# Twelve strips of the dead normalised input as feed-forward tile homes, output rows spread between the next tiles, and a new written-out order

## The chip, the core and the metric

The kernel runs as one program on one core of a Trainium2 chip. The metric is the device time of one execution in microseconds (us). All five engines take part: TensorE (PE, with its weight loads shown as PEld), VectorE (DVE), ScalarE (ACT), GpSimd (POOL), and SyncE (SP), whose queue issues nearly all DMAs.

## The reference

A layer norm without scale feeds an attention block and a gated feed-forward block, and both are added to the input:

```
x = A_x                                   # 1 x 2048 x 512, bf16
xn = (x - mean) / sqrt(var + 1e-5)
q, k, v = split(xn @ A_wqkv)              # 32 heads of 16
o = softmax(q k^T / 4) v                  # 2048 x 2048 scores per head
gate, up = xn @ B_W_gate, xn @ B_W_up     # 512 -> 1792 each
return x + o @ A_wo + (max(gate, 0) * up) @ B_W_down
```

## The kernel before

**Tiling.** The 2048 rows are four chunks of 512 (`c4`), the 32 heads four groups of eight (`gg`), each in two halves (`ee`), the keys sixteen tiles of 128 (`kt`). One key step is one (`c4`, `gg`, `ee`, `kt`): scores of 128 keys against 512 queries for four heads. Of the 512 key steps, 359 go through ScalarE: each gives two units, 718 in all. `score` (L1289) makes the two score tiles of a unit in two PSUM banks, and one activation of 128x1024 (L1365) takes the exponential into a slot of `ring`. There are two such pairs of banks, so the scores of unit u+2 wait for the exponential of unit u. The other 153 key steps are "quads" (`quad`, L1312, placed by the table `QUAD_AT`): VectorE turns the scores into integers that, read as bf16, are approximate exponentials (L1320), and VectorE (L1339) or GpSimd (L1335) makes two shifted copies; all three patterns are multiplied with v. `pv_stream` (L1244) does the products with `v_aug`.

**TensorE's groups.** Nearly every product is split into two row halves of the array (64 rows each) and four column strips of 32. Four matmuls of 64x512 on one half are one group; four weight loads go before it unless the half still holds the same weights. Groups of the two halves run side by side. Line L250 is the helper that emits every one of these matmuls, so they are told apart by their tiles.

**Feed-forward and rows.** `glu` (L992) makes one tile of the feed-forward's hidden layer: a chain of eight groups for `up`, eight for `gate`, and two VectorE operations (L1016, L1020); the result goes to one of `NHS` = 20 slots of `hT`, pool `P_h` (L608). There are 14 such tiles (`ft`) for each chunk, 56 in all. `out_rows` (L1034) makes 128 output rows: a chain of 28 groups over all 14 tiles of the chunk and `W_down`, eight more over the attention output and `W_o`, then the residual. It needs all 14 tiles of its chunk, and frees them when the last of the four rows has read them. The normalised, transposed input `xnT` (128 x 4 x 2048, bf16) is read by all projections; block `c4` of its columns is not read again after the last projection of chunk `c4`. Late in the program `resid` (L1030) keeps two fp32 residuals of the last chunk in it.

**Order.** The jobs (projections, hidden tiles, rows) get due times from a list: all the tiles of a chunk, then its four rows, then the next chunk's tiles:

```
            for ft in range(FT):
                ...
                seq.append(ffn[ft])
                if ft in shared[c4]:
                    seq.append((0, GN, lambda s, c4=c4, ft=ft: glu(c4 + 1, ft, s), W_LEAD + 2))
            seq += rows
```

Half of the tiles of a chunk can be made together with the same tiles of the chunk before it (`shared`), because they use the same weights. But the order in which each engine runs its operations is not worked out when the program is built: `PLAN` is a packed table of `PLAN_OPS` = 8248 entries, which `Graph.run` (L324) unpacks into five queues, with the slot of every tile. `Graph.emit` then sets the semaphore waits. Each engine runs its queue strictly in that order; a wait at the head of a queue holds up all behind it.

Of the kernel before, what the change touches and what calls it, by code (L numbers as in the profile page):

```python
# [16 lines left out]
S = 2048  # L17
# [26 lines left out]
ROW_AT = 20  # L44
XBANKS = (0, 1, 2, 3)
# [82 lines left out]
    "v#>-|tRzVEh^;*em;WkE095*CSm<HqH|`M|cr09qT?N{VqVkBF%{%E!F2OyVSrjJo#C@^#5)-#ki(ELx!R42&{H1*&2Hxz52r$buahFFFHO%CC#9Q)JX4)?UB?Bn-@h~$EIv~rA8_Cs;WrYXK$Nit2"
    "M!^`XNhfIu!$pr-LS8yEID~)F1h<%6rs(#5!hPxRm9Y^lkGYG%5gr*R0~OLCGBU+!z=V64=^WYo$tfJMfyPTKzOG}v;bF$wOvcRc*~FY;Bv>(tiF*u~8(XJvKX15AfN<jhZuJo_&2ULV6kSIO6u07Z"
    "n^5&Yev|jYSj=N$RJvkR9J6dQw^K}4WnknQ2KJbTo4lwq%O)-%r<f?UuuDHk&%DjiSK&Se(yeb+R>Tduswg~lX?yeb(aF4Nkg+hqF8uHqwZ!ZoHmb)Pd?OPS5BUuDmX8s2!)cF~_zloVDiYqnivk~q"  # L130
    "nY1CwOy{3m@(zy-tptie8y<@zOv?m=nS1CyhNEu=B`7eOk-4-{f*<_M5>EDG7OrJlj3<qH<B}A0Uq6ShIT>w0_7VdV7WXDQb<H4KFK}%NhI8+iw?X?D-P<nA;$d8|bq!xzx2@%?Juea2d0J6Ycihz4"
    "iKpttb}qMXVl_42%G{@Q45=jhvlSWL=1(da;oV)g$rSi7X|g-_={ghMqMLJ*p}1~7rOW*c)nvS?_#*193-N&Jm2bY<vBgpM1wl8Rg-!aJs>hOTHhssvVvX}uy4D`TRBeJ=Dnik}C}X4+x2a?83x)z8"
    "P7M7D-$pVbhF-Mp(9NeUoO!Rm(9_&TEIgIe=U=4H*8F8n=~jp=p$ePY^|cgh5n-d%d3{m#82#JSWxiUqOr$1lsdSSV4fZs9w5f$mrt#t2l1_2~v;V<-Ua~WEtC}S<>(DK_7H`2Y3_dto2=#_e`(*Vt"
    "g9R+@W;o|D>5$AY83nqH+ATj!ijo4rE1_gF@^%OKB%gf8QYqHkoEu9rL-W|xonmNwAueE>v%JypMjKYVr8c%?2{)Cy)N9<j!4?E=hFLc`6E;RMR`D1WWsO<B25P)&-fH?P6*#ko0@_pi<kkdX=$0AY"
    "b-5+Vm{;o?c`)6VVKthH$2WqAMUB=5`+#hhw3ZGx!(`SvynFdD{aNE?a4o!<6(z;2ck1!(p?il87~_pKDf!TwTKRHY?HQuc1c<PXTbt^pKioTXnWmT_=C;>JnKGs*-f6>xf;lFcv!dN{GbE;9x6M>u"
    "tGxmi+^fa8t?L>ypru?bvh&uSabXVK-jem|O>Rzxu+2K$8f>l3FN?r5-n!Fl)?9I`7NeRin;X0Yo9|xdypb~dl5M=V+J(jQTxUwEcI)dZ+$){!Ga*kcp}qZ)f7yfok84w%BYZKC*;~J_!F>T9pD$Lg"
    "wKR=+qeb4{Dc*a8A$73TabdB#?_Tq~fZmp;6JjBm8p}iYu<YymJXI&NkD1(em|@|J+X7_G_r|e=PXlpp!?%=(#HU<JN3zp?4wWi>+}2KQ8>O0Xl~f(sUZ(aVEw7$1k1xLH;Kqe{xT0`h;%p~f+y@f="
    "#p_;p@l;sh|G&hSV$NGd7UwJG5s<F|7}p*}VZKms-w?tjWty|PhuKd*OpyhXdll~h=qn<#3DUrn>{8^QZP1{H!?fBMj-cq?QyE3E23c=Ev+<-S)iIUHH1ypZowzl}*=oWjam0RH`z&R)mpDwI*-m<l"
    "-F07|Ft;`PiA9;#$$+)7uNRn3de2=9BdmiRk7BV6Yy}`&q(#PxSMb=*&x}+UozfUkpjaJ1w?-jDoZ4;U)~S*uq%4Y&t;FXmw^OfTQ-I1BptV7t`zB_<CwadlFOM}``;H!TQ?!_AHAhZ!d{$sJG>=UO"
    "d1G(1JfA4^wjMd;d86r_>22g_Vaiy^I@dFhV5&6Ejjp4Z+@^aMF;t8<-d594yhLR-ck95_cb;iKjx_V)v%mzJUGsU*?d;;frr#{In(EdXI=L}cf7WRB=e`4Acp1*BBi%UrvQE+zZg1!O|IYQTpS{dx"  # L140
    "$|c2ys{fY|+}6kKyz0d?-RgE28MgEzPu+w6uRGfN0k;H!ZxG?BdGL$7?I$6yW7*dV?1#Dh3u@)c7oS1c(QXGk=cxuQ+j&6h-r^gM6#U;x*8FCdAKuy4dLFh;>zmGX?)#j=D_LNDBBJ|t@SUU^D|oNG"
    "M@eQ@eZ#68w``rwHXEfvi<LiPH*@+_yo0?-A76~WHm_}JMuA-z!_p~&aCK4lrdEM9=c{hTMrZa<ldK$CM^8M}NNqn`u~d7itaI<-d#ZGCdp^DL$d(S9+jf{4kHI>%GGj?J$jx(H&OFv==beibWBj$w"
    "78R@SS;vST>oWzj$$7kEnRwbf@3So{=Ky95OXf)@^Du9dvMExXS<|k0<X}IAlAVehW?Lud<{+jh7R`IfT(=$E8T`X+XIOfwdXXSEWS_y&1}vCIM1iOJ>_oTb3-hBKZYg`8#b$f-wtZ`&P<-0ME;qcN"
    "W?8gsJ#CF~)`xSjv$|!Ki4?1)n`5H)Lm1hi%mXT)q~c!=S2k+09pR?_e1xYyd9&$m`-j1)`nmT5Q!hmM7jusHsZ>W%itn>jbJnr5lwFbXR39v*5(Zx?Z`((whHU3H;p`pAQk}(k&-)al+T16Uzxcc&"
    "RfzZ(AKAh7nJ)KDNvYgVb!h87$m7PG<dye!D)1ho=wEzNXdB<`r}MtHl4=^TO)p;6<^2>uNeu~KRCV||_LpmkzZsDFzXwh@Kfi|x##s@lx~l4@OK6(^Csp@P!L#(5pL!pe@iZ&^#O;|ikDrJBIxmN5"
    "HyIw}rPmy8`iIeXaYL}@CCkXz)iBM;{=sc}|0W6mIT%9TF{GhwRDQm6LOGnKJ#hi`S>=^LuFA(Mvz@dGeWyQ22CA=YyP#~k7n$CqnbBT%{vHFAOSuPp9hmHNyRHGnpJhl1czXvZ@+yt?%5lBqEqc@K"
    "@_R-$`0WU;wk3kD(v2yNW0SWbxDXIBDo1;b7GB<w?bB-Q9d#?VO&GuTs1t4fJ`RoPZvgPB*F*%hUk^NU?IE`537o-SWpLtorXIj=Ps8zN+UJ=nlmRZTja;7+{Vi~5Y3r40x)<%XeXmzN98`{cN^-j0"
    "fu(`{F5Suacfe8S^3L<yulNl(wMc8P4gG2hurmG8JuJLbLm*xomQu&X;_m{dn{NBjHD;vVzeC}x6wC2>@8r@So!kn<J)Xg@6mqj))2D1m*$32$)E&z^YR$--<((F{UF=7%#r{*^W`WB^)n9=rxgPDQ"
    "F$@^z!spLh&jO=dZ*wFEJR1U(Y>?tmH#HqWacd6enr7=R0b|ywiw~4apw}i8|0^YJlC~U($=(JN-4uw6IC5O?5kC!R<Qj;_tJ^PH2Q(dosa@yM#i(sl`-DB99ZKc8l^^L6{ssoejoj}(hq;xHhVQ6^"
    "_5pg|S+BPP37FY?QgYyj1fXJ)BYg^Rfc%(<&jVNH1S(I%uS3T#j`HgrA#VMU2H#w!2$TX^6=9d%MP>qZS7G_}f_d(=7<26m(DGjP$!Okc4p1W4ec74QbrSd!{oSsj4VwVRdydASi3GN%(=P%CS<j0o"  # L150
    "qTL6w)EqZzLh0SQs^94KFA(XcPe$L*<VWkzepAqE7K&c}2FC}vV`HG6Am~QB%XaR1QsDYv?@RkPd<^>Ncj7jXv(%C@IFk`*=y)IU-v1AvKKx>v&Fn*oeTeSgM<OYN(9`)Ckl3u<!gZ}xk%K6#Vy#gU"
    "I1&1jn=L^UW&8*l)zuDGIZBsR9xyB!`rrEMp{s#r&*D(54m(AV>8qbYI$+wI?(-cnYbag$_xa&Tb2r(Mh;lKpQOjfIQSmve&VC$#`hSwjiNJwgJ5cBMN<iMFXup&%Kl%L-jQ<@d_z8Y*6AAG74x!Sm"
    "uL*G&F^+oEi2YR#CL$9D=Jv+qq2q^AEk6l-h#U`5n2O?7*0d=RJ0I+-yQgywAonsP^`ugKg3E1cj2+gZLqW=9w!GJztl_!Rny2R8gwsHUuP0-G`!3aI*um=Bvh5Q^S~t6!<HC*RC9@JVSsU(PwD@j("
    "p4)=6P-GbTC*70t$y20NHHuP~E{kIpclj6DAGf4<bSi<*UjhH&{PpCLDSkD9;aVrm?}o7Zi0g%{EjBh=*NVb_16iDp@UjqX@!wgOqUBdJ10$;3DEKyD;m?nFmfBQ~>|HBh9b**}7{a~*Hq6ooU}`_S"
    "Z$Z_Y2?v`#IpU(ro10o;Rg(>r-R(%xTMXj=u68THwj?KWJJDcUeQZwB)C{gFK+>Ojc6@f?M=G4MC%*MNx#caDTD$&J7hTozP|EK8MG$HdUnlS%;)Rq3o1BfdeD$bwe9jvM?jGanno|M@RON2gyaHuB"
# [382 lines left out]
def bass_parallel_sum__mha_block__glu_gated_reglu__prompt_kernel(  # L538
# [14 lines left out]
    with ExitStack() as es:  # L553
# [864 lines left out]
```

## Time and profile before

| what | value |
|---|---|
| median of 3 runs (all) | 685.31 us (685.06, 685.31, 686.58) |
| profiled execution, its own time: span from first to last instruction | 684.2 us |
| granted TensorE clock, mean | 0.999 |
| PE busy | 675.6 us (99%), 22262 matmuls, 19654 weight loads |
| ACT busy | 666.8 us (97%), 718 exponentials of 128x1024 |
| DVE busy | 598.5 us (87%) |
| POOL busy | 499.8 us (73%) |
| DMA, mean | 52 GB/s |

The times of the runs are taken without the profiler; the profiled execution is a further one, and its span is 1.1 us below the median of the runs. Busy times of TensorE are pipelined and their ends are modelled, so that 99% does not mean that the array is full. The exponentials of ScalarE also overlap in the profile: the next one begins before the one before has written its end. So the distance between their starts is read below, not their duration.

### The profile page before, as it was taken

What the parts mean: (1) busy time and instruction counts of PE and PEld (TensorE: products, weight loads), DVE (VectorE), ACT (ScalarE), POOL (GpSimd) and SP (SyncE); (2) the same over time, 40 slices, a digit from 0 to 9 for tenths busy, and PEclk for the clock granted to TensorE, in tenths of its full rate; (3) what the DMA queues carried; (4) which work ended last, traced back from release to release, by engine and by line L of the source; (5) the groups of instructions that cost most, each with busy time, mean ns of one, the idle gap of its engine ahead of it and who ended that gap; (6) DMA issues with size and microseconds to landing.
All of it is one profiled execution on the core that took longest, in us unless ns stands there. A gap on an engine that the chain in (4) does not pass through costs nothing.

```text
span 684.2 us, 45020 instructions
## 1 busy us (share of the span) xinstructions
PE 675.6 (99%) x22262; PEld 345.9 (51%) x19654; DVE 598.5 (87%) x1012; ACT 666.8 (97%) x730; POOL 499.8 (73%) x507
## 2 busy tenths in 40 slices
PE   8999999999999999999999999999999999999998
PEld 4455454545555554554444455554554455555543
DVE  9958899999989787999999788889998887988875
ACT  6999999999999999999999999999999999999994
POOL 3323768678688778887587886888878868787792
PEclk9999999999999999999999999999999999999999
DMA  7430220113122021212101022120202012131011
GB/s 216 57 75 12 58 77 27 33 55 91 56 65 66 5 77 34 69 41 63 35 23 31 10 78 63 38 69 5 56 27 61 25 53 62 44 86 42 22 36 54
DMA packets 55940, 35.86 MB, mean 52 GB/s; under 512 B 19336, under 2 KB 51784, under 8 KB 55752
## 3 DMA queue, kind: packets, MB, share of 16 engines
q1 hardware_dynamic: 55464, 32.71, 17.4%
q8 instruction: 164, 2.69, 1.6%
q10 hardware_dynamic: 288, 0.26, 0.1%
q14 instruction: 24, 0.20, 0.1%
HBM read 26.35 MB, written 2.35 MB: 42 GB/s over the span
## 4 chain that ended last, share of the span: by engine, by line
PE 75%; ACT 18%; DVE 5%; issue 1%; DMA 0%; POOL 0%; ACTq 0%
PE ps L250 75%; ACT ring L1365 18%; DVE stats L726 1%; DVE qd L1320 1%; DVE xn_sb L739 1%; DVE v_aug L876 0%; DMA x_sb<-in_A_x_dram 0%; DVE qT L952 0%; DVE mv L727 0%; ACT xn_sb L1164 0%; DVE qd L1339 0%; DVE xnT L780 0%; POOL rstd L721 0%; DVE xnT L1075 0%; DVE kT L869 0%
## 5 line engine op out<-in xcount | busy, mean ns | idle before, releaser
L1365 ACT ACTIVATE ring<-ps 128x1024 bf16<-128x1024 f32 x718 | 660.4, 1141 | 2.9 <-PE ps L250 2.5
L1335 POOL TENSOR_TENSOR qd<-qd,ints 128x512 int32<-128x512 int32 x446 | 450.5, 1041 | 143.8 <-DVE qd L1339 73.2
L250 PE MATMUL ps<-qT,kT 64*32 64x512 bf16 x8192 | 448.7, 374 | 1.3 <-DVE qd L1320 0.4
L1320 DVE TENSOR_SCALAR qd<-ps 128x512 int16<-128x512 f32 x612 | 396.7, 685 | 51.9 <-PE ps L250 49.0
L250 PE MATMUL ps<-qd,v_aug 64*32 64x512 bf16 x3672 | 263.0, 375 | 1.1 <-issue 0.9
L250 PE MATMUL ps<-ring,v_aug 64*32 64x512 bf16 x2872 | 236.5, 374 | 0.1
L1300 PEld LDWEIGHTS <-kT 64*32 64x32 bf16 x7584 | 151.1, 92 | 126.6 <-issue 32.6
L1272 PEld LDWEIGHTS <-v_aug 64*32 64x32 bf16 x4544 | 108.7, 91 | 75.6 <-issue 20.4
L250 PE MATMUL ps<-xnT,wgs 64*32 64x512 bf16 x1792 | 137.6, 374 | 0.0
L250 PE MATMUL ps<-xnT,wus 64*32 64x512 bf16 x1792 | 136.4, 374 | 0.0
L250 PE MATMUL ps<-Wd,hT 64*32 64x512 bf16 x768 | 59.0, 375 | 0.0
L810 PEld LDWEIGHTS <-wgs 64*32 64x32 bf16 x1792 | 43.1, 91 | 31.5 <-issue 7.4
L810 PEld LDWEIGHTS <-wus 64*32 64x32 bf16 x1792 | 43.2, 91 | 29.8 <-issue 7.6
L1339 DVE TENSOR_SCALAR qd<-qd 128x2048 int16<-128x2048 int16 x83 | 56.1, 690 | 2.3 <-PE ps L250 2.2
L810 PEld LDWEIGHTS <-hT 64*32 64x32 bf16 x1792 | 40.2, 92 | 28.2 <-issue 4.2
L250 PE MATMUL ps<-Wv,hT 64*32 64x512 bf16 x512 | 45.7, 375 | 0.0
L250 PE MATMUL ps<-Wk,hT 64*32 64x512 bf16 x512 | 42.8, 375 | 0.4 <-DVE qd L1320 0.3
L1020 DVE SCALAR_TENSOR_TENSOR hT<-ps,up_sb 128x512 bf16<-128x512 f32 x56 | 38.4, 685 | 4.6 <-PE ps L250 4.2
L1016 DVE COPY up_sb<-ps 128x512 f32<-128x512 f32 x56 | 38.4, 685 | 3.1 <-PE ps L250 2.5
L250 PE MATMUL ps<-Wo_p,x_sb 64*32 64x512 bf16 x480 | 40.2, 374 | 0.6 <-issue 0.5
L250 PE MATMUL ps<-xnT,Wq 64*32 64x512 bf16 x480 | 36.2, 375 | 0.0
L250 PE MATMUL ps<-xnT,Wk 64*32 64x512 bf16 x480 | 35.0, 374 | 0.3 <-DVE xnT L780 0.3
(70 smaller groups left out, 263.8 us busy)
## 6 DMA issues: line engine op xcount, KB each, us to landing
rb<-rec_scr SPq DMA_DIRECT2D x31, 256.0 KB
wus<-in_B_W_up_dram SPq DMA_DIRECT2D x38, 128.0 KB, 2.8
wgs<-in_B_W_gate_dram SPq DMA_DIRECT2D x38, 128.0 KB, 3.3
xr_sb<-in_A_x_dram SPq DMA_DIRECT2D x16, 128.0 KB, 2.6
qT<-qf SPq DMA_DIRECT2D x120, 16.0 KB, 2.6
out_dram<-xn_sb SPq DMA_DIRECT2D x14, 128.0 KB, 2.0
x_sb<-in_A_x_dram SPq DMA_DIRECT2D x8, 128.0 KB, 2.8
x_sb<-oT SPq DMA_DIRECT2D x60, 16.0 KB, 2.5
```

Of the source, the lines that this page charges most:

```text
L250: return e.add_instruction(mybir.InstMatmult(name=e.bass.get_next_instruction_name(), engine=mybir.EngineType.PE, ins=[e.lower_ap(x), e.lo ...
L726: G.op("DVE", 580, lambda e, m=m: e.bn_stats(stats[:, m, :], xs(m)), reads=[t_xm[m]], writes=[t_st], prio=pr, order=last_xn if m == 4 else ())
L739: G.op("DVE", 320, lambda e, m=m, t=t_n: e.tensor_scalar(xn_sb[:, t.slot, :], xs(m), mv[:, m, 0:1], rstd[:, m:m + 1], op0=ALU.subtract, op ...
L810: e.ldweights(w()[rows, 32 * j:32 * j + 32], tile_position=(rows.start, 32 * j))
L1016: G.op("DVE", 603, lambda e: e.tensor_copy(up_sb[:, tup.slot, :], bank_of(tu)), reads=[tu], writes=[tup], prio=-590)
L1020: G.op("DVE", 603, lambda e: e.scalar_tensor_tensor(out=hT[:, th.slot, :], in0=bank_of(tg), scalar=0.0, in1=up_sb[:, tup.slot, :], op0=ALU ...
L1272: e.ldweights(vs(j), tile_position=(64 * half, 32 * j))
L1300: e.ldweights(ks(m), tile_position=(64 * half, 32 * m))
L1320: G.op("DVE", 601, lambda e, j=j, tx=tx: e.tensor_scalar(qd[:, tq.slot, 512 * j:512 * j + 512], ps[:, BANK[tx.slot], :], IBIAS[3], 0.0, op ...
L1335: G.op("POOL", POOL_NS / POOL_PIECES + 60, lambda e, x=x, n=n, c=slice(i * m, i * m + m): e.tensor_tensor(x().bitcast(I32)[:, c], raw().bi ...
L1339: G.op("DVE", 600, lambda e, n=n, x=x: e.tensor_scalar(x(), raw(), float(SHIFTS[n + 1]), None, op0=ALU.add), reads=[ti, tq], writes=[t], p ...
L1365: exp_ops[u] = G.op("ACT", 904, lambda e, tr=tr, k0=k0: e.activation(ring[:, tr.slot, :, :], ps[:, 4 * k0:4 * k0 + 2, :], ACTF.Exp, scale= ...
```

## The change

1. Pool `P_h` grows from 20 to 32 slots. The twelve new ones are strips of 128x512 in `xnT`: strip `dt` of block `a`, for `a` = 0, 1, 2. A hidden tile of chunk `c4` may take a strip of a block below `c4`; in the last chunk only some of them, since the residuals will lie in the others. Each strip is guarded by all earlier reads and writes of its block.
2. The four rows of a chunk no longer stand between its tiles and the next chunk's. They are put between the next chunk's tiles, with `ROW_STEP` tiles ahead of each row: one for the rows of the first chunk, two for the second's and the third's.
3. `PLAN` is another table of the same 8248 entries, so the order on all five engines and the slots are new throughout, also where the job list is as before.

The number of operations on each engine is unchanged: 5573 on PE (12 blank fillers among them), 731 on ACT, 1012 on DVE, 503 on POOL, and 429 DMAs on SP. How often TensorE's weights are loaded follows from the order.

```diff
+ROW_STEP = (0, 1, 2, 2)
...
 PLAN_OPS = 8248
 PLAN = (
...
-        P_h = Pool("h", NHS)
+        P_h = Pool("h", NHS + 12)
...
+        def h_of(t):
+
+            if t.slot < NHS:
+                return hT[:, t.slot, :]
+            a, dt = divmod(t.slot - NHS, 4)
+            return xnT[:, dt, 512 * a:512 * a + 512]
...
-            th = t_h[(c4, ft)] = Tile("h", P_h)
+            th = t_h[(c4, ft)] = Tile("h", P_h, list(range(NHS)) + [NHS + 4 * a + dt for a in range(c4) for dt in range(4)
+                                                               if c4 < NB - 1 or a == 2 or dt in TAIL_ACT])
...
-                out=hT[:, th.slot, :], in0=bank_of(tg), scalar=0.0, in1=up_sb[:, tup.slot, :], op0=ALU.max, op1=ALU.mult),
+                out=h_of(th), in0=bank_of(tg), scalar=0.0, in1=up_sb[:, tup.slot, :], op0=ALU.max, op1=ALU.mult),
...
-                    pairs.append(((lambda th=t_h[(c4, ft)]: hT[:, th.slot, 128 * i:128 * i + 128]), (lambda ft=ft: wd_of(ft))))
+                    pairs.append(((lambda th=t_h[(c4, ft)]: h_of(th)[:, 128 * i:128 * i + 128]), (lambda ft=ft: wd_of(ft))))
...
-                seq.append(ffn[ft])
+                tiles.append(ffn[ft])
                 if ft in shared[c4]:
-                    seq.append((0, GN, lambda s, c4=c4, ft=ft: glu(c4 + 1, ft, s), W_LEAD + 2))
-            seq += rows
+                    tiles.append((0, GN, lambda s, c4=c4, ft=ft: glu(c4 + 1, ft, s), W_LEAD + 2))
+            step = ROW_STEP[c4]
+            for n, row in enumerate(behind):
+                seq += tiles[n * step:n * step + step] + [row]
+            seq += tiles[len(behind) * step:]
+            behind = rows
+        seq += behind
...
+        for a in range(3):
+            guard = Tile("xnT")
+            guard.r.extend(o for o in t_xnT[a].w + t_xnT[a].r if o not in resids)
+            P_h.cur[NHS + 4 * a:NHS + 4 * a + 4] = [guard] * 4
```

More of the change, by code (lines that the diff above doesn't have):

```diff
@@ L128 @@
[L128 to L131, printed above, removed]
@@ L216 @@
[L216 to L218 removed]
+    "c-mE52S8127(VYg=ia(a8cGtfNg*O5BNW*)k&-<!i-^onMrJ57N|6<b6dCnL%lPdwDp|=6$-U?N-#F*i|5M$2&v(A>9nbr`<K$<U|NkfAFHwGlzsc|LpGL*#Wh17TzL0JZ={5Y9ek}fPLy@WZ%%%i=F(uM5HTTQ6"
@@ new lines @@
+    "*f7QNhfK|>V(oQU2=rAVize2{fWFs=BK;7xDoF2vVFdhFWCW-sJBa8CdLf9SYytt$LcEw>63{pF5xxmu5dps;i|{QV;M>S8=nKCCQNV}ct0LZ>zC@p58PF2)G1;CWd&`oOGeo?AT#@t_Kto=kJLu;uTEXDW7_uIV"
+    "h(waN6hQ;z71;rZo<t~oi-3i};!~>$L=!9`7Mk3FRUk$nKk0&6vf<Z))=3Q22CGO6B3WA`b`gkpT0JC(Qbk2#EqoIri6#;o*DNF_6T^Ylo#?xorB0>(CK3`|iBE})0@Z+##F3m$j7lT{;!<)uu_Ij|trMuF7)f2A"
+    "yNl8l0wCge(6Az1ul)iEAriQVU+5W<Eh&~Myr}a<rWTY%Q35M98W1Z<79uB5xQLQiB2iUj{_@zE)Ou7nYG$YbzZ4!)Y|#6t5hR0AlN0?k1P>IbEd7{~KNjVWBu_$Z$7=n?YONsaC2Av3pmD;|(}==&JtLt9UBm9x"
@@ new lines @@
+    "h-if<uxJshVbnYo99dk0h0?H0H81%Ov_vC?N-fe5L{<i>hI)d<D<v;u5pY<s<WRbUhJ-K6|7FPO_(b%jA&5gl;gj(P_zsc9M`#Gbu?Bb<dPlCZcry(vdlYI>kcO2xQTC2NO)66XkyUaCi4t-S#VL7Bt`I@Uck~(F"
+    "6B`Pssqv@ex<G*>?MNb*5j8RnHDqgo8Ehy_B`ncJ0w_72)tZ1H25qZhh&{+3L^BeL5VdQtEW?lb14I3fj)Xugn`B#}3o$OWm56ac&%&<8XCojG%Tm2H*c^Ccba0hY8{Z&>hM<irH7}7kR-I@}3?d5DlOo<09fmK7"
+    "^dd2bNc|>a#jrqBM7%$_hS^9Gg`$<IiC;>|8sY?UBEbfM8;g%)$p<V35e6SVoH~_Y1|bWPp{SAL5ULa`BYT*^HfJb0sgI}_k^za!MeGt{GN?t4^rb+eK<1SyU75<Iv_@i*k@AdKlQRjRDTb*OBEf?M2pLc!6$*Vq"
@@ new lines @@
+    "flBTKid1S^K|&z80MyJ_BT*!@#Zp92IEoaXBuEg?|JId&NMcZs1ChuhN)X1mk+7jg;7~ZT%r9LU=Gdad`IHuk$3-dDso6y;AYO>&z@GZc(<l}sCsNoj6!FA^6qn=`m4xDyzQf6dxR|m&+Eqi7Dj`<N4(L;cr7=m>"
+    "5eTERG*l?12~r|uXu8rettg5$bSsL#Rm2ivO(v0<P-K3p7&RwV7ut$SBp->jNSQ>ZP*aFW$I@y=TV09T6rn8<MX4UDR**Xdn(O2}<+~)B!WJYuP;L?_r;;d;k03T>IP7;4{^Wuh*_K1mtY(oh(JNd)u@YrUc*RHK"
+    "wKzCMK`x_6K?53~96^$qHWqLipu|n082Lr~rBAa1E$*axLn8upJSp4=-WVFaq_m@Q3yf5>NVSSKedABD()10~Bu(NE5Tpbz`v7X{R5^p!Sf9G1cDXFM4Qdq*w5FjYpdeR2AQheT1VN%qfuRMTRNGSHh*FIq^P04l"
@@ L221 @@
+    "Cg>t5*nlNetwVAK+T9Q(W6To3W7nW_vBMdhw+Wx%C}PM`&{N<9MT!*smeobvhSW6TFm(~Ts4#?-IyBD{r?B*9T|{jLm=s8PhYCTQ(g}D-QZdKrT*;E~LmDE9Fa&WRBAUP=pzTO4hfRW2(IurL#szE5kz7Md5ey~X"
+    "5VI1-tTES+m{p~qS<!%?4u_c`L)9Rr(WiwBk7JK`kA^3MlcOG16tNg0FOuERa*}=wQI^5=982OA^97@4K<tl@jtVCZ^8{;ViM@!c1X8IQP+BBm&6B#%K#!|uMM^y2D1b115Y<rK%d<*a|6#u23~{Q_$4BWQQz>XP"
+    "W9m~Oisy)d^pQVFM3cb$53^0?x&")
 class Pool:
@@ L1026, in bass_parallel_sum__mha_block__glu_gated_reglu__prompt_kernel @@
         t_oT = {}
-        t_res, kept = {}, {}
+        t_res, kept, resids = {}, {}, []
         glu_last = []
@@ L1075, in out_rows @@
                 o = G.op("DVE", 603, lambda e: e.tensor_tensor(resid(i), bank_of(t, sub), xr_sb[:, txr.slot, :], ALU.add),
-                         reads=[t, txr], writes=[tr] + (t_xnT if i == 0 else []), prio=p1)
+                         reads=[t, txr], writes=[tr] + (t_xnT if i == 0 else []) + [Tile("res%d" % a, P_h, [NHS + 4 * a + i]) for a in range(2)], prio=p1)
+                resids.append(o)
                 if i:
@@ L1098, in bass_parallel_sum__mha_block__glu_gated_reglu__prompt_kernel @@
         shared = [set(range(8, 14)), set(range(2, 8)), set(range(8, 14)), set()]
-        seq = []
+        seq, behind = [], []
         for c4 in range(NB):
-            rows = []
+            rows, tiles = [], []
             for i in range(4) if c4 < NB - 1 else sorted(range(4), key=lambda i: i in TAIL_ACT):
```

181 lines of the change are left out of this document (90 added, 91 removed).

## The prediction

> **What bounds the kernel now.** I read the page's totals, then ScalarE's timeline, because two engines are busy nearly all the time and only one can set the end.
>
> ```profile
> span 684.2 us, 45020 instructions
> PE 675.6 (99%) x22262; PEld 345.9 (51%) x19654; DVE 598.5 (87%) x1012; ACT 666.8 (97%) x730; POOL 499.8 (73%) x507
> PE 75%; ACT 18%; DVE 5%; issue 1%; DMA 0%; POOL 0%; ACTq 0%
> L1365 ACT ACTIVATE ring<-ps 128x1024 bf16<-128x1024 f32 x718 | 660.4, 1141 | 2.9 <-PE ps L250 2.5
> ```
>
> The chain that ended last names PE for 75%, but the exponentials of L1365 are idle for only 2.9 us. The timeline of ScalarE, and the view of that one line, show the pace:
>
> ```profile
> L1365 ACT ACTIVATE ring<-ps x718: 1017/1146/1314, 10.9 to 673.1; 128x1024 bf16<-128x1024 f32 x180
> ...
> 10.91 2.87 ACT L1365 ACTIVATE ring<-ps 128x1024 bf16<-128x1024 f32 x3
> 14.10 146.19 ACT L1365 ACTIVATE ring<-ps 128x1024 bf16<-128x1024 f32 x159 [0.32 <-PE ps L250]
> 160.47 2.85 ACT L1365 ACTIVATE ring<-ps 128x1024 bf16<-128x1024 f32 x3 [0.17 <-PE ps L250]
> 163.63 22.10 ACT L1365 ACTIVATE ring<-ps 128x1024 bf16<-128x1024 f32 x24 [0.31 <-PE ps L250]
> 186.10 38.83 ACT L1365 ACTIVATE ring<-ps 128x1024 bf16<-128x1024 f32 x42 [0.37 <-PE ps L250]
> 225.36 182.36 ACT L1365 ACTIVATE ring<-ps 128x1024 bf16<-128x1024 f32 x198 [0.42 <-PE ps L250]
> 408.64 265.61 ACT L1365 ACTIVATE ring<-ps 128x1024 bf16<-128x1024 f32 x289 [0.92 <-PE ps L250]
> ```
>
> The exponentials overlap: one takes 1.146 us (the median of the first row), but the next starts earlier. A pair of them a little further down lasts 2.05 us from 300.04, so the step between two starts is 2.05 - 1.146 = 0.904 us. This is the shortest step in the trace and also the commonest one. From the first start (10.9) to the last (673.1) there are 717 steps in 662.2 us; at 0.904 they would take 648.2. So the span is made of four parts: 10.9 us before the first exponential, 648.2 of exponentials at full pace, 14.0 of delay spread over the steps, and 11.1 after the last start. The change leaves 718 exponentials, hence the second part. What it can move is the 14.0 us of delay, and a little of the tail. The rest of the argument is what makes a step late.
>
> A step is late when TensorE brings the scores late. This is one step at the level of groups (four matmuls of 64x512 on one half of the array):
>
> ```profile
> 300.04 2.05 ACT L1365 ACTIVATE ring<-ps 128x1024 bf16<-128x1024 f32 x2
> 301.20 0.38 PE L250 MATMUL ps<-ring,v_aug 64*32 64x512 bf16 x4
> 301.20 0.10 PEld L1300 LDWEIGHTS <-kT 64*32 64x32 bf16 x4
> 301.22 0.57 PE L250 MATMUL ps<-qT,kT 64*32 64x512 bf16 x8
> 301.42 0.10 PEld L1300 LDWEIGHTS <-kT 64*32 64x32 bf16 x4
> 301.44 0.38 PE L250 MATMUL ps<-xnT,wgs 64*32 64x512 bf16 x4
> 301.65 0.38 PE L250 MATMUL ps<-ring,v_aug 64*32 64x512 bf16 x4
> 301.87 0.38 PE L250 MATMUL ps<-ring,v_aug 64*32 64x512 bf16 x4
> ```
>
> Groups of one half follow each other every 0.216 us (301.44, 301.65, 301.87), so a step of 0.904 holds 4.2 of them a half. The exponential of 300.04 frees its banks at about 301.2; the two score groups at 301.22 last 0.57 us, to 301.79, and the exponential that needs them is due at 300.04 + 2 x 0.904 = 301.85. Had both halves started at once (0.38 us), 0.25 us would have been left. So TensorE can be late by about one group and no more, and it cannot work ahead, because the banks are not free earlier. The load on TensorE must be even from step to step, not only on average.
>
> **The change part by part.** Two parts, slots and job order, act only through the third, the new queues. So I cost the queues as the built programs have them. All five have the same operations as before, in another order; no time comes from that order itself, only counts, and I price them by the rows.
>
> *Evenness.* I count, in each program, the groups that stand between the scores of one exponential and the scores of the next, on the fuller half. Before: 35 steps with three groups, 572 with four, 106 with five, one with six, and three with fewer. After: 90 with three, 418 with four, 199 with five, five with six, and five with fewer. The sum is the same; the spread is not. I put beside each step of before its delay from the 718 starts of L1365 above: a step with four groups is late by 10 ns on average, with three by 11, with five by 71, and the one with six by 208. (572 x 10.2 + 106 x 71.1 + 35 x 11.1 + 0.2 us gives the 14.0 us back.) After, the same prices give 418 x 10.2 + 199 x 71.1 + 90 x 11.1 + 5 x 208 ns = 20.4 us: 6.4 us more. A few long stalls raise the 71; by medians (43 against 0) the 93 further steps cost 4.0. I take 5.0, between 0 (the 0.25 us above takes every single five) and 6.4.
>
> *Rows.* Where the rows run in one block, the steps are late. These stretches hold 20 steps each, 18.08 us at full pace; the first three hold the rows of the first chunk, then one without, three with the second chunk's:
>
> ```profile
> 214.60:233.60 19.00, 18.72 (x608) 10.01 (x540) 15.35 (x25) 18.57 (x22) 14.67 (x16) 1.00 0.07 19
> 233.60:251.80 18.20, 18.20 (x652) 9.82 (x556) 15.66 (x26) 18.20 (x21) 14.64 (x15) 1.00 0.13 38
> 251.80:270.80 19.00, 18.67 (x652) 9.12 (x572) 14.86 (x24) 18.81 (x21) 15.36 (x16) 1.00 0.25 66
> 270.80:288.90 18.10, 18.10 (x616) 8.90 (x540) 16.86 (x28) 18.10 (x21) 15.91 (x17) 1.00 0.19 57
> 380.60:399.30 18.70, 18.53 (x648) 9.97 (x592) 13.43 (x23) 18.60 (x22) 15.12 (x17) 1.00 0.10 24
> 399.30:418.60 19.30, 18.40 (x664) 10.38 (x564) 15.61 (x26) 18.39 (x21) 13.44 (x14) 1.00 0.23 68
> 418.60:437.20 18.60, 18.57 (x652) 9.83 (x563) 16.62 (x28) 18.58 (x21) 14.06 (x14) 1.00 0.16 42
> ```
>
> Over 18.08 they are late by 0.92, 0.12, 0.92, then 0.02, then 0.62, 1.22 and 0.52 us: 4.3 us in six stretches with rows. The other 9.7 us lie over 30 stretches, 0.32 each; so the surplus of the rows is 4.3 - 6 x 0.32 = 2.4. VectorE has less to do there (13.4 to 16.6 us) while TensorE has more, so spreading the rows should even both out. But 0.9 us of it is no matter of rows: in the chain that ended last stands, amid the rows,
>
> ```profile
> 406.61 0.90 issue
> ```
>
> where TensorE stood still between two weight loads of one group without a semaphore. And the spread is not as wide as the job list suggests: counted in the programs, five stretches of 20 steps hold 160 groups or more (161 to 163) before, and five do after (160 to 163), at other places. I take 1.0 us of gain, between 0 and 2.4. The twelve homes give nothing by themselves: the operation that fills a home waits for TensorE's product alone, for 4.2 of its 4.6 idle us.
>
> ```profile
> L1020 DVE SCALAR_TENSOR_TENSOR hT<-ps,up_sb 128x512 bf16<-128x512 f32 x56 | 38.4, 685 | 4.6 <-PE ps L250 4.2
> ```
>
> *Weight loads.* Another order keeps fewer weights in place: 4,884 groups load theirs before, 5,438 after, so 554 x 4 = 2,216 loads more. By the total row a load is 345.9 us / 19654 = 17.6 ns of PEld's time, 39 us more of 51% busy. The rows above show where it goes: the loads at 301.20 and 301.42 last 0.10 us beside matmuls, and the groups still follow every 0.216. I take 0, up to 2 for loads that come right behind a wait, with nothing to hide them.
>
> The Trainium skill's page "TensorE: Matmul & The Clock Gate", section "The mechanism", says that a weight load overlaps running matmuls only where the row group differs. By it, every reload here would stand in the open on its own half. The trace disagrees: were it so, 4,884 / 2 x 0.10 us would add 244 us to each half's 2,768 x 0.216 = 598, beyond the span of 684.2.
>
> *Tail.* After the last exponential's scores 60 groups stand in the queue before, 61 after, at most 31 on a half either way. The last product with v is the 28th before and the 20th after, so VectorE's last normalisation can start earlier.
>
> ```profile
> 676.94 0.78 DVE L1151 STREAM_TRANSPOSE o_sb<-ps 128x256 f32<-128x256 f32 x2 [2.67 <-PE ps L250]
> 680.88 0.37 ACTq L1162 DMA_DIRECT2D out_dram<-xn_sb  x1
> 681.35 0.60 ACT L1164 ACTIVATE xn_sb<-ps 128x512 bf16<-128x512 f32 x1 [0.51 <-PE ps L250]
> 681.98 0.34 ACTq L1162 DMA_DIRECT2D out_dram<-xn_sb  x1
> ```
>
> At best that saves eight half-slots, 8 x 0.216 / 2 = 0.9 us. Against it, ScalarE now runs both activations and then issues both stores: the last store waits for the issue of the first, 0.37 us. I take 0, from -0.9 to +0.4. The queues' beginnings up to the first exponential are alike: 0.
>
> *Sum.* 5.0 - 1.0 + 0 + 0 = +4.0 us on a span of 684.2, that is 688.2. The median of the runs is 685.3, 1.1 above that span; I keep the 1.1 and forecast 689.3.
>
> **The rivals.**
>
> *Fives are free, rows gain (faster).* If the 0.25 us of room takes each five on its own, the 71 ns belong to waits that happened to fall there, such as this one of 0.73 us for VectorE to empty a bank, and not to the count:
>
> ```profile
> 224.21 0.12 PEld L810 LDWEIGHTS <-hT 64*32 64x32 bf16 x4 [0.73 <-DVE qd L1320]
> ```
>
> Then the 5.0 goes, and the whole row surplus of 2.4 with 0.9 at the tail gives 685.3 - 2.4 - 0.9 = 682.0. It decides from where a step with five groups costs no more than some 15 ns over one with four. For it: PE has room on average, 598 of 662 us a half. Against: lateness is passed on. Pairs of steps that hold nine groups, 1.94 us of work for 1.81, come 213 times after and 133 times before; pairs of ten, 0.35 us too long, four times and once.
>
> *Nothing moves (same).* Row gain and unevenness cancel, or the rows are as dense as before: 685.3, within 1.4 us (0.2%, about what a measurement of this kernel can tell from no change).
>
> *Loads in the open (slower by far).* If the 2,216 loads are not hidden, since they replace kept weights exactly where a wait had just ended: 554 / 2 x 0.10 = 28 us a half, and of the room of 64 us a half little helps a single step; 700 or more. Against: the loads of before are hidden.
>
> **How the numbers follow.** Forecast 0.61, fives free 0.27, nothing moves 0.08, loads in the open 0.04. Faster by over 0.2%: 0.27. Within 0.2%: 0.08. Slower: 0.61 + 0.04 = 0.65. The forecast's own range goes from 687 (evenness 2, rows -1) to 694 (6.4, +2 for loads, +0.4). The range reaches down to the faster rival, 681.0, and up to 695.0.
>
> **What would show it.** In the changed profile: L1365 still 718 times with a shortest step of 0.904; from its first to its last start 666 us in place of 662.2; the delay spread over all stages, also where the job list is unchanged (60 to 180 us); row stretches closer to 18.4 us each; PEld near 385 us. The forecast is wrong if L1365's first-to-last distance is 662 or less, and its step failed at the price of a five if those steps are then no later than the fours.

## The result

| kernel | runs | median us | lowest to highest |
|---|---|---|---|
| before | 4 | 685.19 | 685.06 to 686.58 |
| changed | 4 | 690.76 | 690.0 to 691.57 |

The changed kernel is slower: ratio 1.0078, 95% interval 1.0066 to 1.009. The forecast was 689.3, range 681.0 to 695.0: a loss of 4.0 us, where 5.6 were measured. Time and sign came out; the reasons came out only in part, and the experiments show which part.

The page of the changed kernel, the rows that answer to those of before (the exponentials now stand at L1388, TensorE's matmuls at L259):

```profile
span 688.8 us, 47250 instructions
PE 677.9 (98%) x22259; PEld 384.0 (56%) x21870; DVE 605.9 (88%) x1012; ACT 668.7 (97%) x730; POOL 500.1 (73%) x507
PE 73%; ACT 16%; DVE 8%; POOL 1%; DMA 1%; issue 1%; SPq 0%; DVEq 0%; POOLq 0%
L1388 ACT ACTIVATE ring<-ps 128x1024 bf16<-128x1024 f32 x718 | 662.4, 1070 | 4.5 <-PE ps L259 3.3
```

TensorE and ScalarE look as before; 2,216 weight loads more (21,870 against 19,654) put PEld at 384.0 us. DVE's share of the chain rose from 5% to 8%. The view of the exponentials' line and ScalarE's timeline (start, length, count, in brackets the idle time ahead and its releaser) say where the time is:

```profile
L1388 ACT ACTIVATE ring<-ps x718: 1018/1068/1227, 11.4 to 677.3; 128x1024 bf16<-128x1024 f32 x180
...
11.40 23.51 ACT L1388 ACTIVATE ring<-ps 128x1024 bf16<-128x1024 f32 x25
35.96 1.94 ACT L1388 ACTIVATE ring<-ps 128x1024 bf16<-128x1024 f32 x2 [1.05 <-PE ps L259]
38.05 2.86 ACT L1388 ACTIVATE ring<-ps 128x1024 bf16<-128x1024 f32 x3 [0.15 <-PE ps L259]
41.58 79.17 ACT L1388 ACTIVATE ring<-ps 128x1024 bf16<-128x1024 f32 x86 [0.67 <-PE ps L259]
120.90 113.45 ACT L1388 ACTIVATE ring<-ps 128x1024 bf16<-128x1024 f32 x123
234.89 72.66 ACT L1388 ACTIVATE ring<-ps 128x1024 bf16<-128x1024 f32 x79 [0.54 <-PE ps L259]
308.02 60.10 ACT L1388 ACTIVATE ring<-ps 128x1024 bf16<-128x1024 f32 x65 [0.46 <-PE ps L259]
368.56 309.78 ACT L1388 ACTIVATE ring<-ps 128x1024 bf16<-128x1024 f32 x335 [0.44 <-PE ps L259]
```

The brackets hold only 3.3 us. The rest of the delay is steps that last a little over 0.904 us while the overlapping exponentials still look busy, so it has to be taken from the 718 starts. I cut each profile at the first and last start, and take the delay as the steps' sum less 0.904 each:

| part, us | before | changed | difference |
|---|---|---|---|
| ahead of the first exponential | 10.92 | 11.40 | +0.49 |
| delay, exponentials 0 to 50 | 1.22 | 3.27 | +2.05 |
| delay, the six stretches of 20 with rows (220 to 280, 400 to 460) | 4.30 | 3.07 | -1.23 |
| delay, everywhere else | 8.48 | 11.41 | +2.93 |
| after the last start | 11.11 | 11.43 | +0.33 |

Together +4.6, which is the difference of the spans, 688.8 - 684.2.

The largest single place is new. Here TensorE's and VectorE's timelines of the changed kernel:

```profile
31.96 2.50 DVE L748 TENSOR_SCALAR xn_sb<-hT,mv,rstd 128x512 bf16<-128x512 bf16 x3
34.38 0.68 DVE L878 CAST kT<-ps 128x512 bf16<-128x512 f32 x1
...
33.56 0.41 PE L259 MATMUL ps<-Wv,xnT 64*32 64x512 bf16 x8
35.11 0.38 PE L259 MATMUL ps<-ring,v_aug 64*32 64x512 bf16 x4 [1.14 <-DVE kT L878]
```

VectorE runs three normalisations in a row, 2.50 us, and only then the copy of the keys. The next group in TensorE's queue is held for 1.14 us until that copy ends, and the scores queued behind it come late by the 1.05 us of ScalarE's second row. In the kernel before, this stretch lies inside one row of 159 exponentials without a gap (14.10, 146.19 us long). ScalarE's gap of 0.67 us at 41.58 has another cause in part. TensorE stands still ahead of the fourth weight load of one group, with no semaphore to wait for:

```profile
40.24 0.12 PEld L819 LDWEIGHTS <-Wq 64*32 64x32 bf16 x3
40.84 0.09 PEld L819 LDWEIGHTS <-Wq 64*32 64x32 bf16 x1 [0.47 <-issue]
```

### The profile page after: what moved, and what is told of

It reads as the page before. It is cut to its first block, busy times and chain, and to the rows that moved or that the text cites. A ratio compares the mean times of both kernels' runs of the same rounds, so it can differ in the third digit from the quotient of the medians.

```text
span 688.8 us, 47250 instructions
## 1 busy us (share of the span) xinstructions
PE 677.9 (98%) x22259; PEld 384.0 (56%) x21870; DVE 605.9 (88%) x1012; ACT 668.7 (97%) x730; POOL 500.1 (73%) x507
## 4 chain that ended last, share of the span: by engine, by line
PE 73%; ACT 16%; DVE 8%; POOL 1%; DMA 1%; issue 1%; SPq 0%; DVEq 0%; POOLq 0%
PE ps L259 73%; ACT ring L1388 16%; DVE qd L1343 4%; POOL qd L1358 1%; DVE qd L1362 1%; DVE stats L735 1%; DMA rsum<-o_sb 1%; DVE xn_sb L748 1%; DMA x_sb<-in_A_x_dram 0%; DVE up_sb L1033 0%; DVE hT L1037 0%; DVE o_sb L1221 0%; DVE xnT L789 0%; POOL rstd L730 0%; DVE xn_sb L1086 0%
## 5 line engine op out<-in xcount | busy, mean ns | idle before, releaser
L1388 ACT ACTIVATE ring<-ps 128x1024 bf16<-128x1024 f32 x718 | 662.4, 1070 | 4.5 <-PE ps L259 3.3
L259 PE MATMUL ps<-qT,kT 64*32 64x512 bf16 x8192 | 467.9, 374 | 1.8 <-DVE qd L1343 0.9
L259 PE MATMUL ps<-qd,v_aug 64*32 64x512 bf16 x3672 | 307.8, 374 | 0.6 <-issue 0.2
L259 PE MATMUL ps<-ring,v_aug 64*32 64x512 bf16 x2872 | 250.5, 375 | 1.5 <-DVE kT L878 1.1
L1323 PEld LDWEIGHTS <-kT 64*32 64x32 bf16 x8032 | 165.7, 92 | 110.4 <-issue 22.2
L1295 PEld LDWEIGHTS <-v_aug 64*32 64x32 bf16 x6312 | 151.5, 92 | 83.8 <-issue 13.9
L259 PE MATMUL ps<-xnT,wus 64*32 64x512 bf16 x1792 | 142.6, 374 | 0.0
L259 PE MATMUL ps<-xnT,wgs 64*32 64x512 bf16 x1792 | 139.4, 375 | 0.1
L259 PE MATMUL ps<-Wd,hT 64*32 64x512 bf16 x608 | 54.1, 375 | 0.1
L819 PEld LDWEIGHTS <-hT 64*32 64x32 bf16 x1440 | 34.7, 92 | 17.3 <-issue 3.3
L259 PE MATMUL ps<-Wo_p,x_sb 64*32 64x512 bf16 x480 | 43.6, 375 | 0.5 <-DVE xnT L1037 0.5
L259 PE MATMUL ps<-Wv,hT 64*32 64x512 bf16 x448 | 41.5, 375 | 0.0
L259 PE MATMUL ps<-xnT,Wq 64*32 64x512 bf16 x480 | 38.8, 374 | 0.2 <-issue 0.2
L259 PE MATMUL ps<-Wv,xnT 64*32 64x512 bf16 x576 | 36.7, 374 | 0.1
L259 PE MATMUL ps<-Wk,hT 64*32 64x512 bf16 x384 | 35.0, 375 | 0.0
L259 PE MATMUL ps<-xnT,Wk 64*32 64x512 bf16 x480 | 34.6, 375 | 0.2 <-DVE xnT L789 0.2
```

The lines of the kernel that those rows point to most:

```text
L259: return e.add_instruction(mybir.InstMatmult(name=e.bass.get_next_instruction_name(), engine=mybir.EngineType.PE, ins=[e.lower_ap(x), e.lo ...
L819: e.ldweights(w()[rows, 32 * j:32 * j + 32], tile_position=(rows.start, 32 * j))
L1295: e.ldweights(vs(j), tile_position=(64 * half, 32 * j))
L1323: e.ldweights(ks(m), tile_position=(64 * half, 32 * m))
L1388: exp_ops[u] = G.op("ACT", 904, lambda e, tr=tr, k0=k0: e.activation(ring[:, tr.slot, :, :], ps[:, 4 * k0:4 * k0 + 2, :], ACTF.Exp, scale= ...
```

## Which part of the order costs: splices

A kernel that runs the changed order in some stretches and the order of before in the others should show where the time belongs. `rows_new` takes the changed order only where rows run (exponentials 219 to 335, 394 to 524, and from 556 on), `rest_new` only elsewhere:

```diff
 PLAN_OPS = 8248
 PLAN = (
-    one order throughout
+    entries of one order up to a cut at an exponential, then those of the other that are not there yet, and so on
```

> Built on the changed kernel: the order is that of before, except in the stretches where output rows run (exponentials 219 to 335, 394 to 524 and 556 to the end), which stand in the changed order with the rows spread between the next tiles. Theory A (what costs is the new order as a whole, its less even steps and a few stalls of its own, anywhere; spreading the rows costs nothing by itself): the steps of the two traces, cut at the same places, add up to a span 0.9 us above that of before, so about 686.1. Rival B (spreading the rows is what costs): nearly the whole loss, 690 or more.

> The complement: the changed order outside the row stretches, where the job list is as before, and the order of before (rows in one block) in the row stretches (exponentials 222 to 322, 386 to 515, 567 to the end). Theory A: the steps of the two traces add up to 3.6 us above before, about 688.8. Rival B (spreading the rows costs): 685 to 686.

Measured: `rows_new` 712.65 us, ratio 1.0351 (1.033 to 1.0372); `rest_new` 706.03, 1.0268 (1.0245 to 1.0291). Both are far slower than either pure order, which no theory had said. I blamed the slots that the splice had dealt anew, and cut again with the slots kept:

> As the first kernel of this pair, but at each of the five cuts the buffers of the second order are renamed to what the first order left, so that no tile changes its neighbours (in the first pair 72 and 30 tiles had got other slots, and with them other waits). The changed order stands in the row stretches alone (exponentials 216 to 325, 398 to 524, 570 to the end). Theory A (the order as a whole costs, wherever its steps are late; spreading rows costs nothing by itself): the steps of the two traces, cut at the same places, give a span 1.3 us above that of before. Rival B (spreading the rows costs): 4 us or more above. Rival C (weight loads, 297 groups more than before): 3.0 us above, by 5.6 us for 554.

> The complement, renamed in the same way: the changed order outside the row stretches, before's order with its rows in one block inside them (exponentials 216 to 324, 398 to 532, 570 to the end). Theory A: 3.2 us above before, most of it in the first 50 exponentials. Rival B: within 1 us of before. Rival C (253 groups of loads more): 2.6 us above.

Measured: 711.44 us, 1.037 (1.0354 to 1.0385), and 700.56, 1.0205 (1.0185 to 1.0226). So the slots are not the main part; the cuts are. In `rows_new2`, 24.8 of 40.6 us of delay lie in the five stretches of 20 exponentials that hold a cut (2.4, 4.9, 6.9, 2.3 and 8.3 us). At a cut, operations that one order had brought forward and the other had not yet reached come late or twice as dense, and weights come late, as the waits view of `rows_new2` shows (us in total, times, longest):

```profile
PE ps L255 <- DMA wus<-in_B_W_up_dram: 9.3, 2, 5.9
```

As sums the four runs are a miss. But away from the cuts they tell something: there a stretch mostly keeps the delay of the order that it comes from. From exponential 0 to 160, by twenties, `rows_new2` has .59 .55 .32 .27 .05 .36 .22 .29 and before .60 .54 .24 .34 .06 .35 .24 .28; `rest_new2` has .51 2.73 .26 .30 .35 .55 .31 .72 and the changed kernel .52 2.67 .26 .30 .35 .55 .31 .73. The early loss of 2.05 us comes with the order of that stretch; most late steps in it are fixed by their surroundings and not by chance. About 0.4 us of it is the pause at 40.84: in the profile of `rest_new`, which has no pause there, the step behind it is late by 0.44 us in place of 0.80, and the late steps ahead of it are the same (0.24, 1.19, 0.27). Further on the match is looser: from 240 to 320 `rest_new2` has .21 .23 .23 .31 and before .20 .90 .02 .28.

## The homes alone

`homes_only` keeps the order of before in the changed kernel's code, and puts 18 of the 56 hidden tiles into strips of `xnT`; the changed kernel puts 11 there.

```diff
 PLAN = (
-    order and slots of the changed kernel
+    order of before; a strip for a hidden tile wherever one is free
```

> The changed kernel's twelve further homes in the order of before: 18 of the 56 hidden tiles are put into strips of the normalised input (the changed kernel puts 11 there), all queues stand as before. Theory A (a home costs nothing): 685 to 686. Rival D (reading and writing hidden tiles in those strips, or the waits on their guards, cost): a loss that grows with the tiles, 5.6 x 18 / 11, or at least 2 us of it, 687 to 694.

Measured: 686.25 us, ratio 0.9972 (0.9959 to 0.9984). Its profile:

```profile
span 684.5 us, 45017 instructions
L1377 ACT ACTIVATE ring<-ps 128x1024 bf16<-128x1024 f32 x718 | 661.1, 1131 | 2.4 <-PE ps L248 1.6
```

Delay 14.16 us against 14.00. The homes cost nothing, so the loss is in the order. The ratio says 0.3% faster, but no profile of before was kept from that chip, and beside the one at hand neither span nor delay is shorter. No mechanism for a gain is shown and I claim none.

This run also tells something of the rows, because its order is that of before. In the six stretches with rows its delay is 2.96 us, where before had 4.30. Four of the six agree within 0.01 us; the other two are 0.64 against 0.90 and 0.21 against 1.30. In just these two, the profile of before has pauses of TensorE without a semaphore (0.58 us at 257.4 and 1.27 at 406.2, start to start) that `homes_only` has not. So some 1.3 us of the delay that before has there is no matter of its order, and beside 2.96 the changed kernel's 3.07 shows no gain from spreading the rows (both profiles have one pause of 0.37 us in these stretches).

## Weight loads

`all_loads` is the kernel before with no weights kept: 652 groups more load theirs (5,536 in place of 4,884), nothing is moved. It was run on two chips, the second time beside the changed kernel again.

```diff
-            elif held[o.half] == o.wkey:
+            elif False:
```

> The kernel before with its own order, but weights are never kept: every group of four matmuls loads its weights, 652 groups more (the change had 554 more). Theory A (loads are hidden): 685 to 686. Rival C (the further loads are what costs): in proportion to the loss of the change, 5.6 x 652 / 554 = 6.6 us, 691.8.

> Before's order with no weights kept (652 load groups more) once more, beside the changed kernel on one chip. It lost 15.8 us, and 20.9 us of its trace were pauses of TensorE between two instructions with no semaphore. If these belong to the number of instructions, they come here again: 10 us or more. If they belonged to that chip, this kernel is within 2 us of before.

> The changed kernel once more, on the chip of the other three, as the measure for them. Theory A: 5 to 6 us above before on any chip, since its late steps come from its order. Rival C (weight loads, by the pauses without a semaphore that a kernel with 652 further load groups showed on another chip): the loss goes with that kernel's here, 554/652 of it.

Measured: `all_loads` 704.12 us, ratio 1.0224 (1.0192 to 1.0256); `all_loads2` 691.15, 1.0071 (1.0051 to 1.0091); `after_again` 692.45, 1.0091 (1.0069 to 1.0113). So the loads of 652 groups more cost 15.8 us on one chip and 5.0 on the other. The waits view of before, then of `all_loads`:

```profile
ACT ring L1365 <- PE ps L250: 2.5, 6, 0.9
PE ps L250 <- issue: 1.6, 4, 0.9
```

```profile
ACT ring L1365 <- PE ps L250: 13.9, 26, 2.9
PE ps L250 <- issue: 9.1, 24, 1.3
```

The matmuls wait 24 times for nothing that the profile shows, as in the row `406.61 0.90 issue` of before. The loads themselves are still hidden: groups that got a load follow the group ahead on their half after a median of 0.215 us, as they did without. The loss is not spread over the groups; it sits in pauses of TensorE of up to 1.3 us, often in the middle of a group's four loads.

Is it the loading, or only that TensorE's queue is longer? `all_waits` is the kernel before, and each of the same 652 groups gets four waits on a value that was reached long ago, and no load:

```diff
+                if e == "PE" and o.load is False and last:
+                    for _ in range(4):
+                        eng.wait_ge(*last[0])
                 if e == "PE" and o.load and o not in loaded:
```

> The kernel before; at each of the 652 groups that keep their weights in place, TensorE's queue gets four further waits (on a value that its semaphore reached long ago) where the run with all loads had four weight loads: 2,608 instructions more, and no load more. If the pauses without a semaphore come from how fast TensorE's instructions arrive, they are as many as with all loads: 20 to 38 of over 0.3 us, 8 to 20 us in sum, time 5 us or more above the kernel before (ratio 1.007 to 1.022). If they come from the weight loads, the pauses stay at about 4 and 2.3 us and the ratio is within 0.2% of 1. If the waits cost in themselves, the delay rises evenly in all stretches of 20 exponentials, in place of in few, and no pause is longer than 0.3 us.

Measured: 726.54 us, ratio 1.059 (1.0565 to 1.0615). Page, waits view, and the weight loads' timeline at one pause:

```profile
span 724.7 us, 46321 instructions
```

```profile
ACT ring L1370 <- PE ps L250: 23.2, 53, 1.3
PE ps L250 <- issue: 8.9, 25, 1.1
```

```profile
157.97 0.10 PEld L1277 LDWEIGHTS <-v_aug 64*32 64x32 bf16 x4
159.24 0.09 PEld L1305 LDWEIGHTS <-kT 64*32 64x32 bf16 x4 [1.17 <-issue]
```

The instruction count rose by 1,301: the four waits went as two. The pauses are there (25 of the same kind against 24 with all loads) without one more weight load, so they do not come from loading as such. They are not all of the 40 us, though. The third reading holds in part: the delay rises in 33 of the 36 stretches of 20. Where such a group waited for nothing else, its distance from the group ahead on its half rose from a mean of 0.232 us to 0.270, and over half of the rise stays when the groups behind a pause are left out (the median hardly moves). So the waits cost in themselves, at some of the groups. What makes a pause likelier this run cannot tell.

I count the pauses in one way for all profiles: two instructions of TensorE that start more than 0.3 us apart, the second waiting for no semaphore, from 45 us on (number, and sum of the distances; the expectations above leave the first instruction's own 0.1 us out).

| profile | instructions | pauses | us | delay us |
|---|---|---|---|---|
| before | 45,020 | 4 | 2.7 | 14.0 |
| homes_only | 45,017 | 5 | 2.8 | 14.2 |
| changed | 47,250 | 4 | 1.9 | 17.7 |
| after_again | 47,250 | 12 | 6.4 | 21.3 |
| all_loads | 47,625 | 38 | 24.2 | 34.9 |
| all_loads2 | 47,625 | 20 | 11.0 | 24.7 |
| all_waits | 46,321 | 45 | 28.8 | 54.0 |

In its first profile the changed kernel had no more pauses than before; on the other chip its pauses hold 4.5 us more than in the first. They come on top of what its order costs, and vary from run to run. The number of instructions alone does not decide: 47,250 went with 4 and 12 pauses, 47,625 with 20 and 38, and 46,321 with 45.

Their place is no chance. I counted all of TensorE's records in the order of time, from 0 and in blocks of 256, which is what one fetch of its instructions brings (worked out in the section on the prediction). Of the 128 pauses in the table, 126 stand ahead of the same record of a block: number 190 in six profiles, number 193 in that of before, which has three more matmuls on record at its start. The other two are in `all_loads2`. The pause at 40.84 us stands at 190 too. So nearly all pauses come at the same step from one block to the next, and at some of these crossings only.

## The price of a step with five groups

The forecast's main term was that a step with five groups on a half costs 61 ns more than one with four. `uneven_before` takes the kernel before and moves 154 groups a few places, past the two scores of one exponential, so that there are more fives; `even_after` and `even_before` move groups the other way. No other operation moves, and the number of loads stays. One of the moves of `uneven_before`, in TensorE's queue:

```diff
-up (half 1), ..., score 311 (half 0), score 311 (half 1), up (half 0)
+..., score 311 (half 0), score 311 (half 1), up (half 1), up (half 0)
```

> The kernel before, with 154 of TensorE's groups each moved a few places later, past the two score groups of the next exponential; nothing else is moved, the same 4,884 groups load their weights, the same 2,634 waits stand in TensorE's queue. Steps with five groups rise from 106 to 260, with three from 35 to 92, with four fall from 572 to 361; pairs of steps that hold nine groups rise from 133 to 217 (213 in the changed kernel). Price of a five as predicted (71 ns against 10 for a four): 154 x 61 ns = +9.4 us. Price as the changed kernel's own profile has it (44 against 16): +4.3 us. Fives free, the delays of the fives being waits that fell there: within 0.2% (1.4 us) of the kernel before.

> The changed kernel, with 159 groups each moved a few places past one pair of score groups, so that the counts come near those of the kernel before: 87 steps with five groups in place of 199, 573 with four in place of 418, 47 with three in place of 90; 5,438 groups load, as in the changed kernel. Price of a five as predicted: 112 x 61 ns = 6.8 us less than the changed kernel, so about the time of the kernel before or a little under it (ratio 0.998 to 1.0). Price by the changed kernel's own profile: 3.1 us less, ratio about 1.004. Fives free: as the changed kernel, ratio 1.008 to 1.009; then the loss is in the weight loads, the pauses and the few long waits alone.

> The kernel before with 60 groups moved in the same way, to even it further: 73 steps with five groups in place of 106, 18 with three in place of 35. Price of a five as predicted: 33 x 61 ns = 2.0 us less (ratio 0.997). Price by the changed kernel's profile: 0.9 us less (0.9987). Fives free: 1.000. It is the version most likely to be below both kernels.

Measured: `uneven_before` 696.61 us, ratio 1.0137 (1.0123 to 1.0151), that is +9.2 us; `even_after` 711.07, 1.0345 (1.0328 to 1.0363); `even_before` 693.16, 1.009 (1.0078 to 1.0103).

The first number is the forecast's price almost to the tenth (+9.4), and it would have passed for a proof. The other two, with fewer fives, speak against it: both were to be faster than their source or equal, and both are slower, by 6 us over before and by some 18 over the changed kernel. Pauses explain a part only: there are 8 in `even_before` (4.6 us) and 15 in `even_after` (6.8 us), and 4 in `uneven_before` (2.9 us), as in before. So moving a group costs something that the count does not hold. TensorE's timeline at the move shown above, first before, then `uneven_before`:

```profile
298.18 0.38 PE L250 MATMUL ps<-xnT,wus 64*32 64x512 bf16 x4
298.20 0.38 PE L250 MATMUL ps<-qd,v_aug 64*32 64x512 bf16 x4
298.39 0.60 PE L250 MATMUL ps<-qT,kT 64*32 64x512 bf16 x12
298.69 0.38 PE L250 MATMUL ps<-xnT,wus 64*32 64x512 bf16 x4
```

```profile
301.89 0.65 PE L246 MATMUL ps<-qT,kT 64*32 64x512 bf16 x12
302.38 0.82 PE L246 MATMUL ps<-xnT,wus 64*32 64x512 bf16 x8
302.83 0.38 PE L246 MATMUL ps<-qT,kT 64*32 64x512 bf16 x4
```

The two groups `ps<-xnT,wus` add into one bank, one on each half of the array. The second has a wait for the first, set where a bank goes from one half to the other (754 such waits before, 934 in the changed kernel). Before, the scores stood between them, and the wait was over when it came up: 298.18 and 298.69. Moved, they are neighbours: eight matmuls take 0.82 us, so the second group starts 0.82 - 0.38 = 0.44 us after the first, and its half stands idle meanwhile. The next exponential is late by 0.18 us, where it was on time before.

This can be sorted within one pair of profiles. I took for each move of `uneven_before` the delay of the four steps around it, less that of the same steps before:

| moves that bring a pair of such groups | number | mean ns | sum us |
|---|---|---|---|
| next to each other, or with one group between | 45 | 192 | 8.7 |
| with two groups between | 13 | 93 | 1.2 |
| no closer | 96 | 13 | 1.2 |

Steps not near a move changed by -0.2 us in sum. A step with five groups by itself thus costs some 13 ns (standard error about 9), with a median of 1; the 192 is the price of a wait of one half for the other that comes up too early. `even_before` agrees as far as its numbers go: with steps near a pause left out, 32 moves with a new close wait cost 181 ns each, and the 11 with no such move near them nothing that can be told from 0 (61, standard error 59, median 3). In `even_after`, 68 moves with a new close wait cost 247 each, but the other 71 cost 145 too, and the 34 of those near neither a pause nor a close wait still 84 (standard error 28); what those wait for stays open.

Does the change itself suffer from close waits? It has 32 at a distance of one or two in the queue, before had 15. But the 28 steps that hold them are late by 41 ns on average and 1.1 us in sum, so they explain 1 us of it at most. There most of them seem to fall where a half has time to spare.

## Why the prediction was right, and where it was not

**Floor.** It held: 718 exponentials, and three in a row still take 2.86 us. From first to last start 665.9 us; the prediction said 666, against 662.2 before. PEld was to be near 385 us and is 384.0.

**Evenness, +5.0: the count was right, the price was not, and the cause is only partly this.** Leaving the rows out, the delay rose by 2.05 + 2.93 = 5.0 us, just the term's size. That is luck: 2.05 of it are a few long waits among the first 50 exponentials, most of them behind the normalisations on VectorE and one behind a pause, and have nothing to do with fives. One sign of the prediction also failed. The delay was to grow where the job list is unchanged too, from 60 to 180 us. There the steps with five groups rise from 21 to 38, worth 1.0 us at 61 ns each, but the delay only from 2.45 to 2.64 us (from 2.0, if the step of before that held a pause is left out). The step that failed is "A few long stalls raise the 71": I saw that the mean price held stalls of another origin, and still kept most of it (5.0 of 6.4). In the changed profile itself a five is late by 44 ns and a four by 16; by the moves above a five costs 13. So 93 more fives are worth 93 x 13 = 1.2 to 93 x 28 = 2.6 us, of the 2.93 outside the rows and the start. What the rest is (five steps with six groups at 0.2 us each in place of one, 0.8 us; close waits, up to 1 us) was argued from one profile, not tried.

**Rows, -1.0.** The right size by luck: -1.2 here and -0.6 in the second profile (3.67 us in the same six stretches). The measure was wrong: 1.3 us of the 4.3 of before are pauses that the same order did not meet in `homes_only` (2.96 us). The prediction saw the larger one, 0.9 us that "is no matter of rows", and still counted a gain. These runs show none from spreading the rows.

**Weight loads, 0, up to 2.** The reasoning, that loads hide beside matmuls, held group by group. The term still had the wrong bounds: its failing sentence is "I take 0, up to 2 for loads that come right behind a wait". The loads of 652 groups more on the untouched order cost 5.0 and 15.8 us, for the larger part through pauses that wait for nothing visible. In proportion, those of 554 groups would be 4.3 us on the second chip. In the changed kernel's own two profiles the pauses hold 1.9 and 6.4 us against 2.7 before, so with all pauses put down to the loads, which no run shows, the term was about -1 in the one and +4 in the other.

The Trainium skill's page "Runtime: NRT & Kernel Launch", section "Instruction fetch mechanics", says that the sequencer fetches blocks of 256 instructions while it runs the current one, and that crossing a block is mostly hidden. The page of the profile has a row of instruction fetches (before, then changed: packets, MB, share):

```profile
q8 instruction: 164, 2.69, 1.6%
```

```profile
q8 instruction: 173, 2.83, 1.6%
```

They are TensorE's: 164 x 256 = 41,984, and PE and PEld together count 41,916; the 2,216 loads more brought nine. "Mostly hidden" agrees with before: about 160 blocks and 4 pauses. It fits less well where there are more pauses: 38 at 174 blocks with all loads, 45 at 169 with the added waits. That nearly all pauses stand at one record of 256 ties them to the blocks. Of the 87 pauses over 0.45 us in the seven profiles, each is over 1.17 to 1.61 us after the end of the fetch that had begun last when it started, with a median of 1.40. That a block came too late is the nearest reading; no run tried it, and why it comes late at some crossings, and more often in some programs and on some chips, stays open.

**Tail, 0; beginnings, 0.** +0.33 and +0.49: small, but both on the slow side. "The queues' beginnings up to the first exponential are alike" was true of the counts. The mistake was to stop there: the 40 us behind them, where VectorE normalises, copies keys and serves the quads at once, were priced with the mean of the whole kernel.

**Range.** Its lower end was summed wrongly: 685.3 + 2 - 1 is 686.3, not 687; nothing hangs on it.

**The rivals.** "Fives are free, rows gain" had its first half nearly right (13 ns; it was to decide below 15) and still lost, since the rows gave nothing and the loss came from the start, from other waits and from pauses. "Loads in the open" had the right suspect and the wrong mechanism: not 0.10 us for each group, but pauses, and 700 us came only with all loads on one chip, with the added waits, or at cuts and moved groups. "Nothing moves" is excluded by the interval.

No version here is shown to beat both kernels; `homes_only`, at 0.9972 (0.9959 to 0.9984), is the only one below before, and nothing in its profile says why.

## What to carry to other kernels

Do not price a class of steps by its mean delay: sort the delay first by what each late step waited for, and check that the class still costs when those are taken out. A run that hits a forecast number is no proof of its cause; here the mirror-image run (fewer fives, and slower all the same) undid what the hit seemed to show. Two builds of one order tell which late steps belong to the order and which only happened to fall there. Between two hand-made orders of the same operations, look first at places where one engine gets several operations in a row while another waits for a small one behind them, and at dependent groups that have become neighbours.

## What had not been expected of the hardware

TensorE pauses for 0.3 to 1.7 us (start to start) without waiting for a semaphore, in 126 of 128 cases at the same instruction of a block of 256: 4 times in 684 us with 45,020 instructions, 4 and 12 with 47,250, 20 and 38 times with 47,625, and 45 times with 46,321 of which 1,301 were added waits. The program with all loads lost 5.0 us on one chip and 15.8 on another. A wait that is long satisfied is not free in a full queue either: two instructions of such waits ahead of a group raised the mean distance to the group before from 0.232 to 0.270 us, a part of it by pauses.
